# Weight-conversion steps held near TensorE's count, a logarithm moved behind a relu, and a last output tile in two halves

## The chip, the cores and the metric

The kernel runs on one core of one Trainium2 chip. The metric is the time of one execution on the device, in microseconds (us), as the median over runs. Each engine of the core (TensorE, written PE; VectorE, DVE; ScalarE, ACT; GpSimd, POOL; SyncE, SP) takes its instructions strictly in the order in which the program holds them, and waits at the front of that order until the semaphores that an instruction needs have come.

## The reference

Attention with a threshold, two Fourier transforms, a two-layer MLP and a gated output, for 4 batches of 576 tokens and 512 features:

```python
attn = softmax over the scores >= max - tau          # 8 heads of 64
x = (attn @ v), heads side by side                   # [4, 576, 512]
u = x + real(fft(fft(x, axis=1), axis=2))
un = (u - mean(u)) / sqrt(var(u) + 1e-6)
y = u + maximum(un @ w_ch1, 0) @ w_ch2               # 512 -> 2048 -> 512
gate = sigmoid(causal convolution of y, 5 taps)
out = (gate * (y @ w_val)) @ w_out
```

## The kernel before

All matrix products of the MLP and of the output are done three times over in a 12-bit-mantissa format (high part times high part, high times low, low times high), so each operand stands as a pair `h`, `l`. The two parts come from ScalarE (the high part: a copy or a relu) and VectorE (the low part: the value less the high part).

The MLP runs over tokens in five chunks (512, 384, 512, 512, 384 columns). Chunks 2 and 3 (`FAST`) take the first layer by a seven-product scheme for 2x2 blocks: `g_fast` (L1252) makes eight passes `p`, and a pass has seven products of six matmuls of 256 columns each, into PSUM tiles `x`, `y` and `zz`. The products are tied to each other by small ScalarE and VectorE instructions: `copied` (L1312, ScalarE) takes a partial sum out of PSUM into a scratch half `tmp` before the next product adds to it, `added` (L1316, VectorE) adds a second partial sum, and `relu` (L1323 on ScalarE for `hh`, L1324 on VectorE for `hl`) makes the hidden activations of one half. In the traces `tmp[0]` and `tmp[1]` are both called `cx`, `tmp[2]` is `ct`; some of the `hh`/`hl` pairs lie in tiles called `cx`/`ct` too. Between the products stand the matmuls of the second layer (L1279, three of 512 columns into `c`), taken from a queue by `fill(k)`: eight such groups a pass, four for each hidden block. So a pass has 7 products and 8 groups, 15 steps of 1536 columns each.

`y` and `zz` lie in a pool of two PSUM banks (`ps_f`), and so does `mean`, the column sums for the layer norm (L1037). The norm of the chunk runs beside the passes: squares (L1081), sums on GpSimd (L1086, L1088), `mean`, then Ln and Exp on ScalarE (L1097 and L1098, each behind a table load), then L1100 to L1104 on VectorE, of which L1101 reads `mean`. `advance_norm` takes one step of it where `g_fast` yields, and the Ln only where it yields "long".

`moe2_w_val` and `moe2_w_out` arrive as 64-bit floats and are turned into pairs on the way, beside the passes: each of the pieces that fall into chunks 2 and 3 is loaded by GpSimd's queue into `raw` (L966), converted by L281, L282 (VectorE), L283, L284 (ScalarE), L285, L286, L287 (VectorE) and L291 (GpSimd), and written back to memory from GpSimd's queue (L992). These are the conversion steps.

Where they stand among the instructions of the passes is decided while the program is built: a planner (`Loom`) holds a clock `loom.now[e]` for each engine, every matmul of a pass moves PE's clock on, and at a yield of `g_fast` the main loop lets the planner place all conversion steps whose start is not beyond PE's clock:

```python
                    loom.run(until=loom.now["PE"])
```

The results of a chunk are finished by `g_finish` (L1159: L1164 on VectorE reads `c`, L1165 on GpSimd adds to `res`, L1167 writes to `y_d`); for a chunk ahead of a fast one its four parts are taken one by one at yields of the next chunk's `g_fast`. At the end `emit_out` (L1819) makes 18 output tiles of 128 tokens: twelve matmuls of 512 columns, one ScalarE copy, one write on SP's queue.

Of the kernel before, what the change touches and what calls it, by code (L numbers as in the profile page):

```python
# [12 lines left out]
F32 = mybir.dt.float32  # L13
# [3 lines left out]
AF = mybir.ActivationFunctionType  # L17
# [5 lines left out]
B, H, S, D = 4, 8, 576, 64  # L23
DM = H * D
# [17 lines left out]
FAST = (2, 3)  # L42
# [832 lines left out]
def mlp(tc, right, ps_f, attention, loom, a, u_d, y_d, dram, wide, cw, out):  # L875
    nc = tc.nc
    PE, DVE, ACT, POOL, SP = nc.tensor, nc.vector, nc.scalar, nc.gpsimd, nc.sync
    KB, FB = DM // 128, DFF // 128
# [5 lines left out]
    with ExitStack() as ctx, ExitStack() as top, ExitStack() as top2:  # L884
# [3 lines left out]
        w, got = {}, {}  # L888
# [363 lines left out]
        def g_fast(c):  # L1252

            n = CHUNKS[c]
            m = n // 2
            T = {k: [t.rearrange("p (a b) -> p a b", a=2)[:, :, 0:m] for t in v] for k, v in t_units().items()}
            if c == FAST[0]:
                hb[:] = [[got["h"].tile([128, NM], F32R, tag=f"h{x}", name=f"h{x}") for x in "hl"] for _ in range(2)] + [[units["third"].tile([128, NM], I32, tag=t, name=t).bitcast(F32R) for t in ("cx", "ct")]]
            tmp = [f32(t)[:, i * 256:i * 256 + m] for t in units["cv"][2:] for i in range(2)]
            over, end = [], False  # L1260
            x0 = FAST.index(c) * FB

            def fill(k):
                for _ in range(k):
                    if q:
                        q.popleft()()
                        loom.now["PE"] += 3 * (n / 2.4 + 13.5)

            def group(p, jx, x, o):
                hh, hl = hb[(x0 + x) % 3]  # L1270
                w2h, w2l = w[jx][1]
                first, last = x == 0, x == FB - 1

                def go():
                    if first and o == 0:
                        finish_rest(left[0])
                        ch[c] = [got["ps_c"].tile([128, 512], F32, tag=f"c{o}", name=f"c{o}") for o in range(KB)]
                    for i, (ww, y) in enumerate(((w2h, hh), (w2l, hh), (w2h, hl))):
                        PE.matmul(out=ch[c][o][:, 0:n], lhsT=ww[:, o * 128:(o + 1) * 128], rhs=y[:, 0:n],  # L1279
                                  start=(first and i == 0), stop=(last and i == 2))  # L1280
                    if last:
                        whole.append(o)
                return go

            def product(f, wt, name, first):
                wh, wl = wt
                i = 0
                th, tl = T[name]
                for ww, x in ((wh, th), (wl, th), (wh, tl)):
                    for k in range(2):  # L1290
                        PE.matmul(out=f[:, 0:m], lhsT=ww[:, k * 128:(k + 1) * 128], rhs=x[:, k], start=(first and i == 0),  # L1291
                                  stop=(i == 5), skip_group_check=not first)
                        i += 1
                loom.now["PE"] += 6 * (m / 2.4 + 11.5)
                over.append(name)

            later = []

            def settle():
                while later:  # L1300
                    relu(*later.pop(0))
                while over:
                    name = over.pop(0)
                    if end and c + 1 in FAST:
                        split_block(c + 1, name)

            def taken(ns, e):
                loom.now[e] = max(loom.now[e], loom.now["PE"] - 2000.0) + ns

            def copied(f, t):  # L1310
                taken(act(m), "ACT")
                ACT.activation(t, f[:, 0:m], AF.Copy)  # L1312

            def added(f, t):
                taken(dve(m), "DVE")
                DVE.tensor_tensor(out=t, in0=f[:, 0:m], in1=t, op=ALU.add)  # L1316
                return t

            def relu(src, x, half):
                hh, hl = (t[:, half * m:half * m + m] for t in hb[(x0 + x) % 3])  # L1320
                taken(act(m), "ACT")
                taken(dve(m), "DVE")
                ACT.activation(hh, src, AF.Relu)  # L1323
                DVE.scalar_tensor_tensor(out=hl, in0=src, scalar=0.0, in1=f32(hh), op0=ALU.max, op1=ALU.subtract)  # L1324

            base = (FAST.index(c)) * FB * 2
            for p in range(FB // 2):
                lo, up = w[p][0], w[p + FB // 2][0]
                a11, a12, a22 = ([t[:, i:i + 256] for t in tt] for tt, i in ((lo, 0), (lo, 256), (up, 256)))
                k0 = base + 4 * p  # L1330
                for i in (p, min(p + 2, FB // 2 - 1)):
                    loom.run(lambda: ("combined", i) in loom.done)
                fetch(k0 + 5)
                s2, s1, s3, s4 = ([units["x"][:, (k0 + i) % 5, x:x + 256] for x in (0, 256)] for i in range(4))
                end = p == FB // 2 - 1
                if end and c + 1 in FAST:
                    yield "blocks"
                x = got["ps_h"].tile([128, 512], F32, tag="h", name="x")
                product(x, a11, "b11", True)
                copied(x, tmp[0])  # L1340
                settle()
                yield
                y = ps_f.tile([128, 512], F32, tag="f", name="y")
                product(y, a12, "b21", True)
                added(y, tmp[0])
                later.append((tmp[0], 2 * p, 0))
                yield
                fill(1)
                yield
                product(x, s2, "t2", False)  # L1350
                copied(x, tmp[1])
                settle()
                fetch(k0 + 6)
                yield
                z = ps_f.tile([128, 512], F32, tag="f", name="zz")
                product(z, s1, "t1", True)
                copied(z, tmp[2])
                settle()
                fetch(k0 + 7)
                yield  # L1360
                fill(1)
                yield
                product(x, s3, "t3", False)
                added(x, tmp[2])
                settle()
                fetch(k0 + 8)
                yield "long"
                fill(2)
                relu(tmp[2], 2 * p + 1, 1)
                yield  # L1370
                product(z, s4, "b22", False)
                added(z, tmp[1])
                later.append((tmp[1], 2 * p, 1))
                fetch(k0 + 9)
                yield
                fill(1)
                yield
                product(x, a22, "t4", False)
                settle()
                later.append((x[:, 0:m], 2 * p + 1, 0))  # L1380
                yield
                fill(3)
                yield
                for i, jx in enumerate((p, p + FB // 2)):
                    q.extend(group(p, jx, 2 * p + i, o) for o in range(KB))
            settle()
            rest[:] = [lambda: fill(2 * KB)]

        rest = []
        q, hb, whole, left = deque(), [], [], [iter(())]  # L1390
# [257 lines left out]
        for c in range(1, NCH):  # L1648
            last = c == NCH - 1
            if c in FAST:  # L1650
                norm = g_var(c, POOL)
                for n, m in enumerate(g_fast(c)):
                    if whole and (n % 2 or c > FAST[0]):
                        whole.pop(0)
                        next(left[0], None)
                        continue
                    if n < 12:
                        continue
                    loom.run(until=loom.now["PE"])
                    if m == "blocks":  # L1660
                        while not centred:
                            advance_norm(c, True)
                    advance_norm(c, table=m == "long")
# [66 lines left out]
def gate_out(tc, y_d, w_d, cw, out, ps_f, ypad0, gate0):  # L1730
# [4 lines left out]
    KB = DM // 128  # L1735
    PAD = NK - 1
    with ExitStack() as ctx:
# [79 lines left out]
        flat = out.rearrange("b s f -> (b s) f")  # L1817

        def emit_out(t):  # L1819
            f = ps_o.tile([128, DM], F32, tag="o", name="o")  # L1820
            gh, gl = gv[t * 128 // (2 * S)]
            d = slice(t * 128 % (2 * S), t * 128 % (2 * S) + 128)
            i = 0
            for x, w in ((gh, wo[0]), (gh, wo[1]), (gl, wo[0])):
                for k in range(KB):
                    PE.matmul(out=f, lhsT=x[:, k, d], rhs=w[:, k], start=(i == 0), stop=(i == 3 * KB - 1))  # L1826
                    i += 1
            s = o_p.tile([128, DM], F32, tag="os", name="os")
            ACT.activation(s, f, AF.Copy)
            SP.dma_start(out=flat[t * 128:t * 128 + 128], in_=s)  # L1830

        ps_v = ps_f
        load_y(0)
# [165 lines left out]
```

## Time and profile before

| | |
|---|---|
| median of 3 runs | 847.61 us (847.33 to 848.21) |
| the profiled execution, its own time | 846.86 us |
| its span, first to last instruction | 845.1 us |
| mean granted TensorE clock | 0.998 of full speed |

Busy shares of the span, from the page of the profile: PE 96%, DVE 75%, ACT 53%, POOL 47%. A busy time is what an engine spent inside instructions; where one engine is busy for nearly the whole span, what counts is its idle stretches and what ended each of them, and the stage in which they lie. The stages by time: attention and Fourier transforms to about 400 us, the MLP's chunks to about 740 us (chunk 2 from 492.6, chunk 3 from about 578, chunk 4 from about 673), the gated output to the end.

### The profile page before, as it was taken

Reading aid. Unit: us, or ns where it says so; the run is one execution under the profiler, and the core shown is the slowest. Engines: PE = TensorE matmul, PEld = TensorE weight load, DVE = VectorE, ACT = ScalarE, POOL = GpSimd, SP = SyncE. Lnnn points to the kernel's source line nnn. Section 1 sums busy time; section 2 is a strip of 40 time slices with the busy share of each in tenths; the row PEclk is TensorE's granted clock in tenths of the full one; section 3 lists DMA queues with packets and bytes.
Section 4 is the critical chain, followed back from the end, with each engine's and each line's share of the span. In section 5 each row is a group of like instructions: output and inputs, shape, how many; then the busy total and the mean of one; then the engine's idle time right before and its main releaser. Section 6 shows DMA issues by size and latency. Waiting matters only on the chain.

```text
span 845.1 us, 14968 instructions
## 1 busy us (share of the span) xinstructions
PE 812.5 (96%) x5164; PEld 657.7 (78%) x5164; DVE 633.1 (75%) x1378; ACT 450.5 (53%) x947; POOL 393.1 (47%) x464
## 2 busy tenths in 40 slices
PE   8989999999999999999999999899899999999998
PEld 6555556566665667878899988798799899999986
DVE  7999899898989998798789775756543475829730
ACT  5787787786778866544534254434443223243432
POOL 4557864796788567664242032412421101075421
PEclk9999999999999999999999999999999999999999
DMA  6367365355753459958645557366643141442111
GB/s 217 99 224 236 105 173 185 140 180 174 245 173 140 159 180 377 357 146 325 240 155 219 191 170 253 122 199 225 210 123 109 57 140 38 152 166 82 63 50 62
DMA packets 75435, 145.00 MB, mean 172 GB/s; under 512 B 14296, under 2 KB 24536, under 8 KB 75360
## 3 DMA queue, kind: packets, MB, share of 16 engines
q1 hardware_dynamic: 66736, 116.00, 40.4%
q0 software_dynamic: 8480, 28.05, 10.6%
q8 instruction: 41, 0.67, 0.3%
q14 instruction: 34, 0.28, 0.1%
q10 hardware_dynamic: 144, 0.00, 0.0%
HBM read 104.17 MB, written 39.86 MB: 170 GB/s over the span
## 4 chain that ended last, share of the span: by engine, by line
PE 69%; DVE 19%; ACT 5%; POOL 4%; issue 3%; DVEq 0%; POOLq 0%; ACTq 0%
PE c L1279 10%; PE h L1135 8%; PE c L1152 8%; DVE neg L766 6%; DVE p L783 6%; PE o L1826 5%; PE c L1553 5%; PE h L1517 5%; PE v L1808 5%; PE x L1291 5%; PE s L701 4%; PE f L458 4%; PE zz L1291 2%; PE t L803 2%; ACT e L772 2%
## 5 line engine op out<-in xcount | busy, mean ns | idle before, releaser
L791 POOL TENSOR_SCALAR p<-p,su 128x576 f32<-128x576 f32 x144 | 110.2, 775 | 83.9 <-DVE su L718 74.6
L772 ACT ACTIVATE e<-s,neg 128x576 f32<-128x576 f32 x144 | 102.1, 742 | 50.6 <-DVE neg L766 43.9
L783 DVE SCALAR_TENSOR_TENSOR p<-s,thr,e 128x576 f32<-128x576 f32 x144 | 112.4, 814 | 8.7 <-DVE thr L711 0.5
L766 DVE TENSOR_REDUCE neg<-s 128x1 f32<-128x576 f32 x144 | 102.4, 746 | 5.6 <-PE s L701 5.0
L701 PE MATMUL s<-kt,qt 64*128 64x288 f32 (+1 forms) x640 | 98.3, 438 | 6.9 <-DVE p L783 5.6
L701 PEld LDWEIGHTS s<-kt,qt 64*128 64x128 f32 (+1 forms) x640 | 45.7, 175 | 46.2 <-issue 15.6
L803 PE MATMUL t<-ident,p 128*128 128x128 f32 x464 | 68.9, 280 | 8.9 <-ACT m L820 6.6
L803 PEld LDWEIGHTS t<-ident,p 128*128 128x128 f32 x464 | 50.6, 140 | 30.1 <-issue 13.7
L458 PE MATMUL f<-m,v 128*64 128x320 f32 (+1 forms) x512 | 69.5, 411 | 0.0
L820 ACT ACTIVATE m<-t 128x512 f32<-128x512 f32 x116 | 65.6, 599 | 1.6 <-PE t L803 0.7
L1138 ACT ACTIVATE hh<-h 128x384 fp32r<-128x384 f32 x32 | 15.7, 491 | 81.4 <-PE h L1135 81.3
L291 POOL TENSOR_TENSOR ct<-raw 128x512 fp32r<-128x512 f32 x24 | 26.0, 1083 | 69.6 <-DVE raw L287 40.0
L1165 POOL TENSOR_TENSOR res<-cs,res 128x512 f32<-128x512 f32 (+1 forms) x16 | 19.5, 1243 | 77.9 <-DVE cs L1164 77.9
L458 PEld LDWEIGHTS f<-m,v 128*64 128x64 f32 x512 | 33.8, 137 | 27.3 <-ACT m L820 3.5
L1782 DVE SCALAR_TENSOR_TENSOR acc<-ypad,cw,acc 128x288 f32<-128x288 f32 x96 | 42.9, 513 | 0.0
L1152 PE MATMUL c<-hl,w1h 128*128 128x384 f32 x128 | 42.8, 334 | 0.0
L1152 PE MATMUL c<-hh,w1l 128*128 128x384 f32 x128 | 42.8, 334 | 0.0
L1152 PE MATMUL c<-hh,w1h 128*128 128x384 f32 x128 | 42.8, 334 | 0.0
L1811 DVE TENSOR_TENSOR gvf<-v,gate 128x288 f32<-128x288 f32 x30 | 13.6, 454 | 36.7 <-PE v L1808 35.5
L1312 ACT ACTIVATE cx<-x 128x256 f32<-128x256 f32 x32 | 12.2, 382 | 49.7 <-PE x L1291 49.7
L1139 DVE SCALAR_TENSOR_TENSOR hl<-h,hh 128x384 fp32r<-128x384 f32 x32 | 17.8, 555 | 27.6 <-ACT hh L1138 27.6
L283 ACT ACTIVATE cx<-cx,wide_bias 128x512 int32<-128x512 int32 x40 | 28.9, 722 | 14.3 <-DVE cx L281 14.2
(349 smaller groups left out, 2240.9 us busy)
## 6 DMA issues: line engine op xcount, KB each, us to landing
raw<-in_moe_w_ch POOLq DMA_DIRECT2D x32, 512.0 KB, 5.9
mlp_xu<-s SPq DMA_DIRECT2D x64, 256.0 KB, 3.7
qt<-in_q SPq DMA_DIRECT2D x15, 576.0 KB, 5.2
kt<-in_k SPq DMA_DIRECT2D x15, 432.0 KB, 3.7
s<-raw SPq DMA_DIRECT2D x12, 512.0 KB, 2.6
ypad<-y_d SPq DMA_DIRECT2D x16, 288.0 KB, 3.1
out<-os SPq DMA_DIRECT2D x18, 256.0 KB, 2.0
v<-in_v SPq DMA_DIRECT2D x16, 256.0 KB, 2.6
```

The source lines that it names most:

```text
L458: PE.matmul(out=f[h * 64:h * 64 + 64, 0:n], lhsT=w, rhs=r, start=(t == 0), stop=(t == 4))
L701: PE.matmul(out=s[o, c, 0:HALF], lhsT=qt[w, hh, q], rhs=kt[w, 2 if h == 2 and hh else hh], start=True, stop=True)
L766: DVE.tensor_reduce(out=neg[u][:, j, 0:1], in_=sc[g][:, :, 0:HALF], axis=AX.XY, op=ALU.max, negate=True)
L772: ACT.activation(e, sc[g][:, :, 0:HALF], AF.Exp, bias=neg[u][:, j, 0:1], scale=1.0)
L783: DVE.scalar_tensor_tensor(out=p_view(g).rearrange("p (a b) -> p a b", a=2), in0=sc.pop(g)[:, :, 0:HALF], scalar=thr[u][:, j:j + 1], in1=e ...
L791: POOL.tensor_scalar(out=v, in0=v, scalar1=ssum[u][:, j:j + 1], scalar2=1.0, op0=ALU.mult, op1=ALU.mult)
L803: PE.matmul(out=f[:, t, :], lhsT=pv[:, t * 128:(t + 1) * 128], rhs=ident, is_transpose=True, start=(t == 0), stop=(t == 3))
L820: ACT.activation(o, fv, AF.Copy)
L1135: PE.matmul(out=f[:, 0:n], lhsT=ww[:, k * 128:(k + 1) * 128], rhs=x[:, k, 0:n], start=(i == 0), stop=(i == 3 * KB - 1))
L1152: PE.matmul(out=ch[c][o][:, 0:n], lhsT=ww[:, o * 128:(o + 1) * 128], rhs=x, start=(at_ == 0 and i == 0), stop=(at_ == FB - 1 and i == 2))
L1279: PE.matmul(out=ch[c][o][:, 0:n], lhsT=ww[:, o * 128:(o + 1) * 128], rhs=y[:, 0:n], start=(first and i == 0), stop=(last and i == 2))
L1291: PE.matmul(out=f[:, 0:m], lhsT=ww[:, k * 128:(k + 1) * 128], rhs=x[:, k], start=(first and i == 0), stop=(i == 5), skip_group_check=not f ...
```

## The change

Three edits. First, at each yield of `g_fast` that takes a step of the norm or lets the planner run, the planner's clocks of DVE, ACT and POOL are moved up to no earlier than PE's clock less 700 ns, so that conversion steps are not placed as if those engines had been free long before; and the four parts of the chunk-1 finish are taken at the yields numbered 5, 6, 7, 8 of the first fast chunk, where they were taken at 1, 3, 5, 7. Second, the yield called "long", at which the Ln may be placed, moves behind the relu of `tmp[2]`. Third, the last output tile is made in two halves of 256 columns, each with its own copy and write.

```diff
                 added(x, tmp[2])
                 settle()
                 fetch(k0 + 8)
-                yield "long"
+                yield
                 fill(2)
                 relu(tmp[2], 2 * p + 1, 1)
-                yield
+                yield "long"
                 product(z, s4, "b22", False)
...
                 for n, m in enumerate(g_fast(c)):
-                    if whole and (n % 2 or c > FAST[0]):
+                    if whole and (n > 4 or c > FAST[0]):
                         whole.pop(0)
                         next(left[0], None)
                         continue
+                    for e in ("DVE", "ACT", "POOL"):
+                        loom.now[e] = max(loom.now[e], loom.now["PE"] - 700.0)
                     if n < 12:
                         continue
                     loom.run(until=loom.now["PE"])
...
         def emit_out(t):
-            f = ps_o.tile([128, DM], F32, tag="o", name="o")
             gh, gl = gv[t * 128 // (2 * S)]
             d = slice(t * 128 % (2 * S), t * 128 % (2 * S) + 128)
-            i = 0
-            for x, w in ((gh, wo[0]), (gh, wo[1]), (gl, wo[0])):
-                for k in range(KB):
-                    PE.matmul(out=f, lhsT=x[:, k, d], rhs=w[:, k], start=(i == 0), stop=(i == 3 * KB - 1))
-                    i += 1
             s = o_p.tile([128, DM], F32, tag="os", name="os")
-            ACT.activation(s, f, AF.Copy)
-            SP.dma_start(out=flat[t * 128:t * 128 + 128], in_=s)
+            n = DM // 2 if t == B * S // 128 - 1 else DM
+            for r in (slice(r, r + n) for r in range(0, DM, n)):
+                f = ps_o.tile([128, DM], F32, tag="o", name="o")[:, 0:n]
+                i = 0
+                for x, w in ((gh, wo[0]), (gh, wo[1]), (gl, wo[0])):
+                    for k in range(KB):
+                        PE.matmul(out=f, lhsT=x[:, k, d], rhs=w[:, k, r], start=(i == 0), stop=(i == 3 * KB - 1))
+                        i += 1
+                ACT.activation(s[:, r], f, AF.Copy)
+                SP.dma_start(out=flat[t * 128:t * 128 + 128, r], in_=s[:, r])
```

The order of the built programs shows what this moves. The first place (place A) is VectorE at the start of chunk 2, pass 0, where the four L1164 finish chunk 1:

```order
 L1316 TENSOR_TENSOR cx<-y,cx 128x256
+L1324 SCALAR_TENSOR_TENSOR hl<-cx,hh 128x256
 L1164 TENSOR_TENSOR cs<-c_5568,nr 128x384
-L1324 SCALAR_TENSOR_TENSOR hl<-cx,hh 128x256
+L1316 TENSOR_TENSOR ct<-x,ct 128x256
 L1164 TENSOR_TENSOR cs<-c_5569,nr 128x384
+L1324 SCALAR_TENSOR_TENSOR hl<-ct,hh 128x256
 L1164 TENSOR_TENSOR cs<-c_5570,nr 128x384
-L1316 TENSOR_TENSOR ct<-x,ct 128x256
-L1324 SCALAR_TENSOR_TENSOR hl<-ct,hh 128x256
+L1316 TENSOR_TENSOR cx<-zz,cx 128x256
 L1164 TENSOR_TENSOR cs<-c_5571,nr 128x384
```

Before, three L1164 stood ahead of the first `ct<-x`; now one does, and each instruction of the pass stands between two L1164.

The second place (place B) is ScalarE and VectorE in the pass of chunk 2 that holds the Ln. ScalarE before:

```order
L1312 ACTIVATE ct<-zz 128x256
L283 ACTIVATE cx<-cx,wide_bias 128x512
L284 ACTIVATE ct<-ct 128x512
L1097 ACT_TABLE_LOAD
L1097 ACTIVATE nr<-mean,eps 128x512
L1098 ACT_TABLE_LOAD
L1098 ACTIVATE nr<-nr 128x512
L1323 ACTIVATE hh<-ct 128x256
L1323 ACTIVATE hh<-cx 128x256
L1312 ACTIVATE cx<-x 128x256
```

ScalarE now:

```order
L1312 ACTIVATE ct<-zz 128x256
L1323 ACTIVATE hh<-ct 128x256
L1097 ACT_TABLE_LOAD
L1097 ACTIVATE nr<-mean,eps 128x512
L1098 ACT_TABLE_LOAD
L1098 ACTIVATE nr<-nr 128x512
L283 ACTIVATE cx<-cx,wide_bias 128x512
L1323 ACTIVATE hh<-cx 128x256
L284 ACTIVATE ct<-ct 128x512
L1312 ACTIVATE cx<-x 128x256
```

`hh<-ct` has passed the Ln block, and the two conversion steps have gone from in front of the block to behind it. VectorE in the same pass, before:

```order
L1316 TENSOR_TENSOR ct<-x,ct 128x256
L1324 SCALAR_TENSOR_TENSOR hl<-ct,hh 128x256
L285 SCALAR_TENSOR_TENSOR cx<-raw,cx 128x512
L286 SCALAR_TENSOR_TENSOR raw<-raw,ct 128x512
L287 TENSOR_SCALAR raw<-cx 128x512
L1316 TENSOR_TENSOR cx<-zz,cx 128x256
L1100 TENSOR_TENSOR cs<-nr 128x512
L1101 SCALAR_TENSOR_TENSOR cs<-mean,eps,cs 128x512
L1324 SCALAR_TENSOR_TENSOR hl<-cx,hh 128x256
```

VectorE now:

```order
L1316 TENSOR_TENSOR ct<-x,ct 128x256
L1324 SCALAR_TENSOR_TENSOR hl<-ct,hh 128x256
L281 TENSOR_SCALAR cx<-raw 128x512
L1316 TENSOR_TENSOR cx<-zz,cx 128x256
L282 TENSOR_SCALAR ct<-raw 128x512
L1324 SCALAR_TENSOR_TENSOR hl<-cx,hh 128x256
L285 SCALAR_TENSOR_TENSOR cx<-raw,cx 128x512
L286 SCALAR_TENSOR_TENSOR raw<-raw,ct 128x512
L1100 TENSOR_TENSOR cs<-nr 128x512
L1101 SCALAR_TENSOR_TENSOR cs<-mean,eps,cs 128x512
```

`cx<-zz` has now one conversion step in front of it in place of three, and L1100 and L1101 stand behind the relu `hl<-cx` and two conversion steps.

The third place (place C) is ScalarE in pass 1 of chunk 3, where L1081 takes the chunk's squares:

```order
 L1323 ACTIVATE cx<-x 128x256
-L283 ACTIVATE cx<-cx,wide_bias 128x512
-L284 ACTIVATE ct<-ct 128x512
 L1081 ACTIVATE cs<-z 128x512
 L1312 ACTIVATE cx<-x 128x256
 L1323 ACTIVATE hh<-cx 128x256
+L283 ACTIVATE cx<-cx,wide_bias 128x512
+L284 ACTIVATE ct<-ct 128x512
 L1312 ACTIVATE ct<-zz 128x256
```

The two conversion steps have moved from in front of the copy `cx<-x` to in front of the copy `ct<-zz`.

## Rows read from the trace of the kernel before

**Rows 1.** The page: each engine's busy time, share of the span, instructions.
```profile
PE 812.5 (96%) x5164; PEld 657.7 (78%) x5164; DVE 633.1 (75%) x1378; ACT 450.5 (53%) x947; POOL 393.1 (47%) x464
```

**Rows 2.** TensorE's waits, 430 to 680 us: total, times, longest (us).
```profile
PE x L1291 <- ACT cx L1312: 2.9, 1, 2.9
PE c L1279 <- DVE hl L1324: 1.1, 1, 1.1
PE y L1291 <- DVE cx L1316: 1.0, 1, 1.0
PE x L1291 <- DVE ct L1316: 0.9, 1, 0.9
PE c L1279 <- ACT hh L1323: 0.4, 1, 0.4
PE zz L1291 <- ACT ct L1312: 0.3, 1, 0.3
```

**Rows 3.** Busy time by stretch: PE, PEld, DVE, ACT, POOL (instructions), PEclk, DMA, GB/s.
```profile
530.00:550.00 20.00, 17.64 (x107) 15.04 (x106) 15.48 (x28) 7.49 (x19) 9.57 (x11) 1.00 0.40 120
590.00:610.00 20.00, 17.14 (x99) 15.04 (x98) 10.09 (x20) 8.54 (x20) 9.46 (x9) 0.91 0.65 211
610.00:630.00 20.00, 20.00 (x128) 18.06 (x128) 10.68 (x22) 9.00 (x18) 5.10 (x6) 1.00 0.38 112
```

**Rows 4.** Timeline, VectorE at place A: start, length, line, tiles, [idle before].
```profile
495.63 0.95 DVE L1324 SCALAR_TENSOR_TENSOR hl<-cx,hh 128x256 fp32r<-128x256 f32 x1 [0.43 <-ACT hh L1323]
496.50 1.01 DVE L1164 TENSOR_TENSOR cs<-c,nr 128x384 f32<-128x384 f32 x2
497.43 0.41 DVE L1316 TENSOR_TENSOR ct<-x,ct 128x256 f32<-128x256 f32 x1
```

**Rows 5.** Timeline at place B: ScalarE, VectorE, and TensorE's `y`.
```profile
527.00 1.28 ACT L1097 ACT_TABLE_LOAD   x1
...
530.29 0.63 ACT L1098 ACTIVATE nr<-nr 128x512 f32<-128x512 f32 x1
530.83 0.40 ACT L1323 ACTIVATE hh<-ct 128x256 fp32r<-128x256 f32 x1
...
531.27 0.43 DVE L1324 SCALAR_TENSOR_TENSOR hl<-ct,hh 128x256 fp32r<-128x256 f32 x1 [4.45 <-ACT hh L1323]
531.61 0.69 DVE L285 SCALAR_TENSOR_TENSOR cx<-raw,cx 128x512 int32<-128x512 int32 x1
...
533.15 0.42 DVE L1316 TENSOR_TENSOR cx<-zz,cx 128x256 f32<-128x256 f32 x1
...
535.00 0.75 DVE L1101 SCALAR_TENSOR_TENSOR cs<-mean,eps,cs 128x512 f32<-128x512 f32 x1
...
533.62 0.51 PE L1291 MATMUL y<-raw,w0h 128*128 128x256 f32 x2 [1.03 <-DVE cx L1316]
```

**Rows 6.** Timeline at place C: VectorE, ScalarE, and TensorE's `x`.
```profile
592.30 1.49 DVE L282 TENSOR_SCALAR ct<-raw 128x512 int32<-128x512 int32 x1
...
592.41 0.72 ACT L283 ACTIVATE cx<-cx,wide_bias 128x512 int32<-128x512 int32 x1 [2.75 <-DVE cx L281]
593.82 0.63 ACT L284 ACTIVATE ct<-ct 128x512 f32<-128x512 int32 x1 [0.69 <-DVE ct L282]
...
594.88 0.36 ACT L1312 ACTIVATE cx<-x 128x256 f32<-128x256 f32 x1
...
595.29 0.75 PE L1291 MATMUL x<-unh,mlp_xu 128*128 128x256 f32 x4 [2.86 <-ACT cx L1312]
```

**Rows 7.** The last output tile: its copy in the timeline, and the writes' landing.
```profile
841.48 0.60 ACT L1829 ACTIVATE os<-o 128x512 f32<-128x512 f32 x1 [2.19 <-PE o L1826]
...
DMA to landing us min/median/max: 2.0/2.0/2.2
```

**Rows 8.** Line L281, 490 to 675 us: duration ns min/median/max, and idle before it.
```profile
L281 DVE TENSOR_SCALAR cx<-raw x8: 417/422/812, 489.6 to 607.3; 128x512 int32<-128x512 int32 x8
...
  DMA moe_w_val_h<-cx: 2.0, 1
```

## The prediction

> **What bounds the kernel now.** I read the busy shares first: TensorE is busy 96% of the span [rows 1], so only what makes it wait, or run at a lower clock, can move the time. Next its waits in the two fast chunks [rows 2]: six, of 2.9, 1.1, 1.0, 0.9, 0.4 and 0.3 us, together 6.6. The table by stretch puts a price on them [rows 3]. A regular stretch of 20 us holds 128 matmuls, so one is worth 0.156 us. A pass has 66 of them (7 products of 6, 8 groups of 3), so it takes 10.3 us, and one of its 15 steps 0.70. The stretch 530 to 550 holds 107, which is 21 x 0.156 = 3.3 us lost, where the waits show 1.0 + 1.1 + 0.3 = 2.4: a stall costs some 0.3 us beyond what is shown. The stretch 590 to 610 holds 99, which is 4.5 us lost for one wait of 2.9; there the granted clock reads 0.91 where the others read 1.00, so about 18% of it ran at the lower level (1.2 of 2.4 GHz), worth 9% of 20 us = 1.8. At place A the waits of 0.9 and 0.4, with 0.3 each, make 1.9 us. The three places lose 9.7 us in all. The rest of the change stands where TensorE does not wait, apart from the end.
>
> **Place A, start of chunk 2.** TensorE's `x` waited 0.9 [rows 2] for `ct<-x`, which ran from 497.43 to 497.84 [rows 4]; so it was due at about 497.0. Ahead of it VectorE held `hl<-cx`, 0.95, with GpSimd's L1165 at work beside it (the same form takes 0.43 [rows 5]), and three L1164, two of them 1.01 together [rows 4]. Now `hl<-cx` comes first, at 495.63 and without L1165 beside it, as no L1164 has yet fed GpSimd: it ends at 496.06, one L1164 (0.5) at 496.6, `ct<-x` (0.41) at 497.0. The 0.9 goes. The second wait has two L1164 and a contended `hl<-ct` behind `ct<-x` still ahead of `cx<-zz`, and so of `hh<-cx`. It was 0.4; I take 0.65, as an L1164 of 0.5 has come between, less half of it in slack. Left: 0.65 + 0.3 = 0.95, gain 0.9. Bounds: from nothing (the two L1164 at 0.95 each, as contended as the relu) to all 1.9.
>
> **Place B, the Ln in chunk 2.** ScalarE's Ln block runs from 527.00, and `hh<-ct` behind it begins at 530.83: 3.83 us [rows 5]. VectorE idles 4.45 us for it, does the conversion steps L285 to L287 from 531.61, and only then `cx<-zz` at 533.15, for which `y` waits 1.03 until 533.62 [rows 5]; so `y` was due at 532.6. Now `hh<-ct` and `cx<-zz` need nothing of the block. `hh<-ct` goes when TensorE has left the buffer that it writes: that is where the product `zz` begins, seven steps ahead of `y`, 532.6 - 7 x 0.70 = 527.7. Behind its 0.40 the block begins at 527.9 (neighbours overlap by 0.1 to 0.2) and lets the next instruction go at 531.7. `cx<-zz` runs near 529, so the 1.03 goes. L283 (0.72 [rows 6]) and `hh<-cx` (0.40) end at 532.8, `hl<-cx` (0.43) at 533.2. TensorE wants `hh` one step behind `y`, at 533.3, and `hl` at 533.8: no wait, with 0.5 of slack.
>
> What is late next is L1101, since `mean` keeps one of the two banks of `ps_f` until it has been read, and the next `zz` needs that bank. TensorE wants it three steps behind `y`, at 534.7. Behind `hl<-cx` stand L285 and L286 (0.69 for the first [rows 5]; 1.2 for both, as they overlap a little: the three before took 533.15 - 531.61 = 1.54, the last a short one), then L1100, at 0.7 like L285, then L1101, 0.75 [rows 5]: 533.2 + 1.2 + 0.65 + 0.75 = 535.8. A new wait of 1.1 therefore, with the 0.3 a loss of 1.4 in place of 3.3: gain 1.9. L1100 takes two inputs from memory, and such an operation has been seen to double beside GpSimd (0.43 to 0.95, [rows 4, 5]); then L1101 comes 0.8 later. Bounds: nothing (the wait grows to the old loss) to 2.9 (GpSimd idle, small overlaps).
>
> The block's length decides here. The two loads and two activations fit into the 3.83 us, since from the first load (1.28) to the second activation (530.29) only 3.29 pass [rows 5]. The Trainium skill (ScalarE: Activation LUTs, "What ACT_TABLE_LOAD costs") gives each switch of tables a load of about 1283 ns and then a drain of about 1380. The load agrees with the row. Two drains would not fit between those two starts, so the trace speaks against them, and I use the row; by the Trainium skill the block would end 2.76 later, and both Ln would lose about that much.
>
> **The Ln of chunk 3.** It made no wait before. The same shift applies, with no conversion steps left in front of L1100. Against place B the chain is shorter by L283, L285 and L286, about 1.2 at VectorE, which is the wait of place B: the loss is 0.1, between 0 and 0.8.
>
> **Place C, chunk 3.** The copy `cx<-x` began at 594.88, and `x` waited 2.86 until 595.29 [rows 6]: due at 592.43. Ahead of it stood L283, for which ScalarE had idled 2.75 from 589.66, L284, held by L282 (1.49), and L1081. Without the first two ScalarE is free early: L1081 and the copy (0.36) end near 591.5, before 592.43. The wait of 2.86 goes, and I take the clock's fall to go with it: the stretch 530 to 550 had a stall of 1.06 and read 1.00 [rows 2, 3], this one had 2.86 and read 0.91. Now L284 stands ahead of `ct<-zz`. It ended at 594.45, the copy behind it ends at 594.8, and the product that needs it is due three steps behind 592.43, at 594.5: a wait of 0.3, of which I count 0.4. Gain 4.5 - 0.4 = 4.1. Bounds: 2.3 (that wait at 2, with no fall of the clock) to 4.5.
>
> **The last tile.** Before: twelve matmuls of 512, a copy of 0.60, a write that lands in 2.0 to 2.2 [rows 7]. Now the last copy has 256 columns, 0.36 like the copy in rows 6, and the first half's copy and write run beside TensorE's second half. The second write goes through the same queue behind the first; its landing I leave as it is. Gain 0.2, between 0 (a landing that grows by as much) and 0.5 (the lesser write is quicker).
>
> **The order's other moves.** Clamping the clocks lets conversion steps go later, not more often. GpSimd's loads (L966) and writes (L992) and its step L291 go with them; SP's queue holds no conversion work. I cost them at nothing: the cover is the slack of the pieces, whose loads wait in `raw`. The one place where it was thin is the rival that ends slower.
>
> **Sum.** 0.9 + 1.9 - 0.1 + 4.1 + 0.2 = 7.0 us. The profiled execution took 846.86, which gives 839.9; it lies 0.75 below the median of 847.61, from which the same gain gives **840.6 us**.
>
> **The rivals.** About 0.2%, or 1.7 us, is what a measurement of this kernel can tell from no change.
>
> 1. At place C the wait only moves: L282, 1.49 because GpSimd works beside it, holds L284 later by as much, and the wait at `zz` is 1.8 with the clock's fall again: 1.8 + 0.3 + 1.8 = 3.9 in place of 0.4. Gain 3.5, **844.1**. For it: L282 now runs later among other steps. Against: the wait would begin from a point where TensorE has not idled yet, and be shorter than 2.86.
>
> 2. At place B L1100 and the steps ahead of it double beside GpSimd, and `zz` waits 3.0, as much as was lost before: gain 5.1, **842.5**. For it: GpSimd is busy 9.57 of 20 us in this stretch [rows 3]. Against: none of VectorE's steps in rows 5 was doubled.
>
> 3. No change: the block is longer in its new place. If each load took its 1.28 twice, `hl<-cx` would come 2.6 later at both Ln, less the slack of 0.5 in the first, a loss of 2.1 + 2.6 and some stalls: gain about 1.7, **845.9**. Against: the length in rows 5 was taken with the same neighbours. The drain that the Trainium skill names, above, would end at about the same time.
>
> 4. The gain is given back: something behind chunk 3 ends at a fixed time, a transfer or a chain of VectorE's, and TensorE waits there for what it won. About **847**. Against: TensorE is the bound to the end, and no wait in rows 2 is on a transfer.
>
> 5. Slower: the conversion steps wait on transfers. L281 once idled 2.0 us for the write of the piece before [rows 8], harmlessly, since VectorE had time. Now L281 is placed late and stands just ahead of `added` steps such as `cx<-zz`; a write that has not landed would hold the whole pass. Eight conversions fall into the two chunks [rows 8]. To be slower by 1.7 us it must eat the 7.0 as well, 8.7 in all: from 1.1 us of held TensorE per conversion on. At 1.5 each the loss is 12, **852.6**. For it: the 2.0 is seen. Against: once in eight, and a later L281 leaves the write more time.
>
> **How the numbers follow.** Chances: my forecast 0.63, with its own range 838.5 to 842 (from the bounds at A and B); rival 1 0.12; rival 2 0.11; rival 3 0.03; rival 4 0.05; rival 5 0.06. The range goes down to 837.8 (B at 2.9, A and C whole, a tail of 0.5: 9.8 gained) and up to 844.2, which takes in rivals 1 and 2 and leaves out 3 to 5, 0.14, and the outer ends of the bounds. Faster by over 0.2%: the forecast and rivals 1 and 2, 0.86; within 0.2%: rivals 3 and 4, 0.08; slower: rival 5, 0.06.
>
> **What would show it.** Right: among TensorE's waits the 2.9 on the copy `cx`, the 1.0 on `cx<-zz` and the 0.9 on `ct<-x` are gone; a new one of about 1.1 at `zz` for L1101, one near 0.65 at place A, one near 0.3 for `ct<-zz` at place C; the stretches at places B and C hold about 119 and 125 matmuls, with a granted clock of 1.00 in the second; the last copy takes 0.36. Wrong: TensorE's waits name `hl` or `hh` behind the Ln block (rival 3), L281 idles for transfers ahead of an `added` (rival 5), the clock falls again at place C (rival 1), or the waits go and the span keeps its length through new ones behind 680 us (rival 4).

## The result and the profile after

The changed kernel takes 840.02 us (median of 5 runs, 839.31 to 842.30) where the kernel before takes 847.61: the ratio is 0.9913, 95% interval 0.9899 to 0.9928. The forecast was 840.6, in a range of 837.8 to 844.2. The profiled execution is the slowest of the five, 842.30, with a span of 840.5 us: it lost 2.3 us near 220 us, in the attention stage, where its granted clock read 0.50 from 220 to 222 us and 0.68 to 224; that stage's order of work is the same in both kernels. So I don't compare spans, but the moments at which TensorE begins the same matmul in the two traces:

| TensorE's matmul | before, us | after, us | after less before |
|---|---|---|---|
| `y`, last pair, first pass of chunk 2 | 493.73 | 496.87 | +3.14 |
| `zz`, behind place A | 505.80 | 507.78 | +1.98 |
| `c<-cx`, ahead of place B | 530.33 | 532.11 | +1.78 |
| `zz`, behind place B | 548.71 | 548.74 | +0.03 |
| `y`, ahead of place C | 589.22 | 589.20 | -0.02 |
| `c<-cx`, behind place C | 599.99 | 595.85 | -4.14 |
| first `h` of chunk 4 | 673.06 | 669.08 | -3.98 |
| `o` of an output tile | 832.86 | 828.87 | -3.99 |
| end of the span | 845.1 | 840.5 | -4.6 |

From 3.14 behind to 4.6 ahead are 7.7 us: 1.16 at place A and 0.2 more by 515 us, 1.75 at B, 4.1 at C, 0.6 at the end, less 0.16 in the pass of chunk 3's Ln; nothing between 673 and 832 us.

Of TensorE's waits from 430 to 680 us two are left [rows 2]:

```profile
PE zz L1291 <- DVE cs L1101: 1.2, 1, 1.2
PE zz L1291 <- ACT ct L1312: 0.3, 1, 0.3
```

The stretches of places B and C (columns as in [rows 3]) hold 118 and 123 matmuls, 11 and 24 more, and the second has its clock back:

```profile
530.00:550.00 20.00, 18.84 (x118) 16.76 (x117) 14.02 (x25) 10.31 (x22) 6.67 (x7) 1.00 0.44 133
...
590.00:610.00 20.00, 19.72 (x123) 17.37 (x122) 14.02 (x27) 9.23 (x21) 9.28 (x9) 1.00 0.71 233
```

Place A in the timeline of VectorE [rows 4]: the relu takes 0.43, `ct<-x` stands behind one L1164, and the relu `hl<-ct` takes 0.56. The relu `hl<-cx` behind them takes 0.85, and TensorE's `c<-hl` starts 0.54 behind the matmul ahead of it, where 0.24 is usual: a stall of 0.3, too short for the list above (VectorE, then TensorE):

```profile
498.77 0.43 DVE L1324 SCALAR_TENSOR_TENSOR hl<-cx,hh 128x256 fp32r<-128x256 f32 x1 [0.90 <-ACT hh L1323]
499.11 0.55 DVE L1164 TENSOR_TENSOR cs<-c,nr 128x384 f32<-128x384 f32 x1
499.58 0.42 DVE L1316 TENSOR_TENSOR ct<-x,ct 128x256 f32<-128x256 f32 x1
...
500.48 0.56 DVE L1324 SCALAR_TENSOR_TENSOR hl<-ct,hh 128x256 fp32r<-128x256 f32 x1
...
502.33 0.85 DVE L1324 SCALAR_TENSOR_TENSOR hl<-cx,hh 128x256 fp32r<-128x256 f32 x1
...
502.69 0.40 PE L1279 MATMUL c<-hh,w1l 128*128 128x512 f32 x1
503.23 0.50 PE L1279 MATMUL c<-hl,w1h 128*128 128x512 f32 x1
```

Place B [rows 5], ScalarE, VectorE and TensorE: the block gives way to L283 at 533.53, `hl<-cx` runs at 534.58, L1101 ends at 537.60, and `zz` begins behind it:

```profile
533.53 0.71 ACT L283 ACTIVATE cx<-cx,wide_bias 128x512 int32<-128x512 int32 x1
534.14 0.40 ACT L1323 ACTIVATE hh<-cx 128x256 fp32r<-128x256 f32 x1
...
534.58 0.43 DVE L1324 SCALAR_TENSOR_TENSOR hl<-cx,hh 128x256 fp32r<-128x256 f32 x1 [3.43 <-ACT hh L1323]
...
536.85 0.75 DVE L1101 SCALAR_TENSOR_TENSOR cs<-mean,eps,cs 128x512 f32<-128x512 f32 x1
...
537.65 0.74 PE L1291 MATMUL zz<-unh,mlp_xu 128*128 128x256 f32 x4 [1.16 <-DVE cs L1101]
```

The prediction gave L1100 0.7 us. In the kernel before it had taken 1.48, beside L291 on GpSimd, in lines that [rows 5] leaves out:

```profile
533.48 1.48 DVE L1100 TENSOR_TENSOR cs<-nr 128x512 f32<-128x512 f32 x1
...
533.38 1.04 POOL L291 TENSOR_TENSOR ct<-raw 128x512 fp32r<-128x512 f32 x1 [14.28 <-DVE raw L287]
```

In the changed kernel it takes 0.69, and L291 comes 2 us behind it:

```profile
536.12 0.69 DVE L1100 TENSOR_TENSOR cs<-nr 128x512 f32<-128x512 f32 x1
...
538.74 1.09 POOL L291 TENSOR_TENSOR ct<-raw 128x512 fp32r<-128x512 f32 x1 [15.19 <-ACT cx L1323]
```

Place C [rows 6]: L284 still waits for L282, but now only `ct<-zz` stands behind it:

```profile
593.83 0.63 ACT L284 ACTIVATE ct<-ct 128x512 f32<-128x512 int32 x1 [0.71 <-DVE ct L282]
594.37 0.36 ACT L1312 ACTIVATE ct<-zz 128x256 f32<-128x256 f32 x1
...
594.79 0.75 PE L1291 MATMUL zz<-unh,mlp_xu 128*128 128x256 f32 x4 [0.28 <-ACT ct L1312]
```

The last copy [rows 7] begins 3.0 us before the span's end, where the one before began 3.6 before it:

```profile
837.51 0.38 ACT L1833 ACTIVATE os<-o 128x256 f32<-128x256 f32 x1 [0.99 <-PE o L1831]
```

### The profile page after: what moved, and what is told of

Same layout as the page of the kernel before. It is cut to its first block, busy times and chain, and to the rows that moved or that the text cites. A ratio compares the mean times of both kernels' runs of the same rounds, so it can differ in the third digit from the quotient of the medians.

```text
span 840.5 us, 14996 instructions
## 1 busy us (share of the span) xinstructions
PE 812.9 (97%) x5176; PEld 659.3 (78%) x5176; DVE 634.9 (76%) x1378; ACT 451.1 (54%) x948; POOL 394.3 (47%) x464
## 4 chain that ended last, share of the span: by engine, by line
PE 70%; DVE 17%; ACT 5%; POOL 3%; issue 3%; DMA 1%; SPq 0%; DVEq 0%; ACTq 0%; POOLq 0%
PE c L1279 10%; PE h L1135 8%; PE c L1152 8%; DVE neg L766 6%; DVE p L783 6%; PE o L1831 5%; PE h L1517 5%; PE c L1553 5%; PE v L1810 5%; PE x L1291 5%; PE s L701 4%; PE f L458 4%; ACT e L772 3%; PE zz L1291 2%; PE t L803 2%
## 5 line engine op out<-in xcount | busy, mean ns | idle before, releaser
L291 POOL TENSOR_TENSOR ct<-raw 128x512 fp32r<-128x512 f32 x24 | 25.7, 1073 | 71.9 <-DVE raw L287 49.8
L283 ACT ACTIVATE cx<-cx,wide_bias 128x512 int32<-128x512 int32 x40 | 28.9, 722 | 11.7 <-DVE cx L281 11.7
L1279 PE MATMUL c<-hh,w1h 128*128 128x512 f32 x88 | 34.8, 395 | 0.0
```

## The experiments

My theory at the start: each place is paid by one edit, A by the yields 5 to 8, C by the clamp, the end by the halves; and at B either the clamp or the Ln's move would have been enough, and the two together get in each other's way. The rival: the Ln's move is what pays at B, and the wait for L1101 is its price. The kernel before ran again beside the experiments, with medians of 848.11 us (e_n4 to e_noln), 847.72 (b_late to t_onewrite) and 847.24 (the last three); the ratios are to these, while the expected times start from 847.6.

**e_n4: only the finish's yields**, on the kernel before.

```diff
-                    if whole and (n % 2 or c > FAST[0]):
+                    if whole and (n > 4 or c > FAST[0]):
```

> Only the four L1164 of chunk 1 go to the later yields. Theory: place A is theirs alone, so this kernel gains what the changed kernel gained there, 1.4 us (846.2), with both waits of place A gone and those of places B and C as before (1.03, 1.06, 2.86). Rival: place A was also helped by the clamped clocks, and the second wait, 0.4, stays: gain 0.7, 846.9.

Measured: 846.95 us (ratio 0.9990, interval 0.998 to 1.000); in the trace 1.16 us are gained at place A, as in the changed kernel, but 0.5 given back 13 us later. L281 idles 2.0 for its transfer as in [rows 8], L282 0.6 more, and ScalarE's L284 holds the copy `cx<-x`, which TensorE now wants earlier:

```profile
511.22 0.43 DVE L281 TENSOR_SCALAR cx<-raw 128x512 int32<-128x512 int32 x1 [1.98 <-DMA moe_w_val_h<-cx]
512.25 0.43 DVE L282 TENSOR_SCALAR ct<-raw 128x512 int32<-128x512 int32 x1 [0.60 <-DMA moe_w_val_l<-ct]
...
512.71 0.63 ACT L284 ACTIVATE ct<-ct 128x512 f32<-128x512 int32 x1 [0.30 <-DVE ct L282]
513.25 0.36 ACT L1312 ACTIVATE cx<-x 128x256 f32<-128x256 f32 x1
...
513.66 0.74 PE L1291 MATMUL x<-unh,mlp_xu 128*128 128x256 f32 x4 [0.44 <-ACT cx L1312]
```

So the rival's size was right (0.65 net in the trace) and its reason wrong: place A needs no clamp, but the clamp keeps what A has won. This is my rival 5 in small, 0.4 us of held TensorE at one conversion.

**e_clamp: only the clamp**, on the kernel before.

```diff
+                    for e in ("DVE", "ACT", "POOL"):
+                        loom.now[e] = max(loom.now[e], loom.now["PE"] - 700.0)
```

> Only the clocks are clamped. Theory: place C is the clamp's alone (gain 4.0), and at place B it is the conversion steps that did the harm, not the place of the Ln: with L283 and L284 no longer in front, the block begins 1.3 us earlier, hh<-ct follows it at 529.6, cx<-zz comes by 531.2 and L1101 ends by 533.2, all before TensorE asks, so all 3.3 us of place B are gained as well: 7.3 in all, 840.3, with no wait at y, c or zz there. Rival: the block in front of hh<-ct still makes y or c wait, some 1.5 us of it: 841.8 or more, with such a wait among TensorE's.

Measured: 840.70 us (0.9913, 0.9899 to 0.9927). Place B gained 3.2 of 3.3, with no wait at `y`, `c` or `zz`: VectorE has `cx<-zz` at 531.83 and L1101 at 533.22, in a trace that runs 1.6 us behind that of before at this point.

```profile
530.72 0.40 ACT L1323 ACTIVATE hh<-ct 128x256 fp32r<-128x256 f32 x1
...
531.83 0.42 DVE L1316 TENSOR_TENSOR cx<-zz,cx 128x256 f32<-128x256 f32 x1
...
533.22 0.75 DVE L1101 SCALAR_TENSOR_TENSOR cs<-mean,eps,cs 128x512 f32<-128x512 f32 x1
```

Place C gained its 4.1. But 0.95 went between the two, in waits that I had not expected, told under e_noln. By its ratio the clamp alone is as good as the whole change, 0.9913 each; by the traces it gains 6.6 us from chunk 2 to the end, where the whole change gains 7.7.

**e_ln: only the Ln's move**, on the kernel before.

```diff
-                yield "long"
+                yield
                 fill(2)
                 relu(tmp[2], 2 * p + 1, 1)
-                yield
+                yield "long"
```

> Only the Ln moves behind the relu. Theory: L283 and L284 stay in front of the block and so out of the way of hh<-cx behind it; hl<-cx ends at 532.6 and L1101 at 533.95, before zz asks at 534.7: place B is gained whole, 3.3 us, 844.3, with place A and C as before. Rival (the wait for the bank of mean comes of the Ln's new place as such): zz waits 1.2 for L1101 as in the changed kernel, gain 1.75, 845.9.

Measured: 843.44 us (0.9947, 0.9935 to 0.9960); place B gained 3.2 and its waits are gone, and places A and C are as before. TensorE's waits from 430 to 690 us:

```profile
PE x L1291 <- ACT cx L1312: 2.9, 1, 2.9
PE x L1291 <- DVE ct L1316: 0.9, 1, 0.9
PE c L1279 <- ACT hh L1323: 0.4, 1, 0.4
```

The rival falls: with the Ln behind the relu, L1101 started at 533.17 here and nothing waited for it. The wait of 1.16 in the changed kernel comes of both edits: the clamp puts L283 behind the block and L285, L286 behind `hl<-cx`, where the moved Ln has no slack left for them.

**e_noln: the changed kernel without the Ln's move.**

```diff
-                yield
+                yield "long"
                 fill(2)
                 relu(tmp[2], 2 * p + 1, 1)
-                yield "long"
+                yield
```

> The changed kernel without the move of the Ln. Theory: the move costs 1.5 us beside the clamp (two good edits that get in each other's way): place B has no wait left, and the time is 1.5 to 1.8 under the changed kernel's 840.0, 838.4; ratio to before 0.989. Rival: without the move y, c or zz wait 1 us or more at place B, and the time is 840.0 or above.

Measured: 839.71 us (0.9901, 0.9889 to 0.9914). Place B is gained whole, 3.15 in place of 1.75, but one pass later 0.95 is lost: the next chunk's `mean` stands where it stood before, four steps ahead of its place in the changed kernel, and TensorE, now earlier, meets it while L1026 and L1027 still make its two parts.

```profile
542.36 0.50 PE L1037 MATMUL mean<-cs,ones 128*128 128x512 f32 x1 [0.21 <-ACT cs L1026]
...
543.08 0.50 PE L1037 MATMUL mean<-cs,ones 128*128 128x512 f32 x1 [0.22 <-DVE cs L1027]
```

Two waits shown with 0.2 each cost 0.95 by the matmuls' start times. So the Ln's move had an effect that I had not seen in the order: as every later step of the norm goes with it, it also gave `mean` its distance.

**b_late: e_noln with a later `mean`.**

```diff
-            yield 2500.0 if c > FAST[0] else 4500.0
+            yield 4500.0
             mu = col_mean(parts)
```

> The changed kernel without the move of the Ln, and the step from the sums to mean made 4500 ns long in the fast chunks (was 2500). Theory: of the 1.55 us that the version without the move gained at place B, 0.95 was given back one pass later, where mean now stood right behind the sums' two parts and TensorE waited for L1026 and L1027; three steps later it finds them done: 0.95 under that version, 838.7, and none of the two waits at mean. Rival: a later mean holds its bank longer and another product waits for it, so that the time stays at 839.7.

Measured: 838.94 us (0.9891, 0.9878 to 0.9904). The waits at `mean` are gone, and from chunk 2 to the end this trace gains 9.0 us on that of before, where the changed kernel gains 7.7 and e_noln 8.4. By the traces it beats these two; by the medians it is 1.1 us under the changed kernel, with intervals that overlap.

**x_bank: the changed kernel, with `mean` copied out of PSUM ahead of the Ln.**

```diff
             yield "table"
+            if c in FAST:
+                v = scratch(n)
+                DVE.tensor_copy(v, var)
             ACT.activation(r, var, AF.Ln, bias=eps[:, 0:1])
+            if c in FAST:
+                var = v
```

> The changed kernel, in which VectorE copies mean out of PSUM just ahead of the Ln, and L1101 reads the copy. Theory: what is left at place B is the bank of ps_f that mean holds until L1101; with the copy ended by 531.5 the zz product, due at 536.5, gets its bank early, the wait of 1.16 for L1101 goes, and the time is 1.3 to 1.5 under the changed kernel's: 838.6, with no wait in its place. Rival: the late Ln block makes something else late as well (hl<-x or cx<-y behind L1100 and L1101 on VectorE), another wait of about 1 comes up in that pass, and the time stays at 839.5 to 840.

Measured: 839.51 us (0.9902, 0.9888 to 0.9917). The wait for L1101 is gone, and TensorE comes out of place B 1.35 us earlier than in the changed kernel; so it was the bank. Then 0.95 is lost again by 546 us, so that the rival's time held, by another instruction than it named: VectorE's relu `hl<-ct`, 0.43 in the kernel before, takes 3.24 with GpSimd's sums beside it, and `cx<-zz` and all behind it come late (VectorE, GpSimd and the weight load that waits at the end of the chain):

```profile
539.23 3.24 DVE L1329 SCALAR_TENSOR_TENSOR hl<-ct,hh 128x256 fp32r<-128x256 f32 x1 [0.55 <-ACT hh L1328]
542.40 0.41 DVE L1321 TENSOR_TENSOR cx<-zz,cx 128x256 f32<-128x256 f32 x1
...
539.62 2.56 POOL L1046 TENSOR_TENSOR cs<-z 128x512 f32<-128x512 f32 x2
...
543.32 0.19 PEld L1284 LDWEIGHTS c<-cx,w1h 128*128 128x128 f32 x1 [0.32 <-ACT cx L1328]
```

The relu ends at 542.47, just behind the two sums (542.18). The Trainium skill (SBUF — State Buffer, "SBUF: two separate sides") says that a VectorE instruction with two inputs from SBUF and a GpSimd one that reads SBUF don't share but exclude each other for a whole instruction, and that the one that starts first goes first. The end of the relu agrees; its start does not, since the record has it 0.39 ahead of the sums and it still waited for both. In the changed kernel the same relu took 3.15 and nobody waited, as I read it because TensorE was late from its wait for L1101: of the 1.35 that x_bank won there, 0.95 had been cover.

```profile
541.68 3.15 DVE L1324 SCALAR_TENSOR_TENSOR hl<-ct,hh 128x256 fp32r<-128x256 f32 x1 [0.64 <-ACT hh L1323]
```

That L1046 is the cause is read from the records, and they don't all agree. In e_ln the sums are done by 535.7, and this relu, at 538.91, takes 0.42. But in e_noln it takes 0.43 in the middle of the sums (GpSimd, then VectorE), so that standing beside them is not enough, and what decides stays open:

```profile
536.90 2.90 POOL L1046 TENSOR_TENSOR cs<-z 128x512 f32<-128x512 f32 x2
...
538.22 0.43 DVE L1324 SCALAR_TENSOR_TENSOR hl<-ct,hh 128x256 fp32r<-128x256 f32 x1 [0.68 <-ACT hh L1323]
```

**e_tail: only the halves**, on the kernel before (the third edit of the change, its line of sizes shown), and **t_onewrite**: the changed kernel, with one write behind both copies.

```diff
+            n = DM // 2 if t == B * S // 128 - 1 else DM
+            for r in (slice(r, r + n) for r in range(0, DM, n)):
```

```diff
                 ACT.activation(s[:, r], f, AF.Copy)
-                SP.dma_start(out=flat[t * 128:t * 128 + 128, r], in_=s[:, r])
+            SP.dma_start(out=flat[t * 128:t * 128 + 128], in_=s)
```

> Only the last tile in two halves. Theory: from the start of the last copy to the end of the span 2.99 us as in the changed kernel (3.62 before): 0.22 for the copy and 0.4 for the write of half the size; 847.0. Rival: the write of a half takes as long as that of a whole tile and the 0.4 was chance: 3.4 us, 847.4.

> The changed kernel with both halves' copies, but one write of the whole tile behind the second. Theory: the write's size is worth 0.4, so from the start of the last copy to the end of the span 3.4 us in place of 2.99; 840.4. Rival: only the copy counts, 3.0 us, and the time is the changed kernel's.

Measured: e_tail 847.21 us (0.9991, 0.9981 to 1.0002), t_onewrite 840.12 (0.9909, 0.9896 to 0.9922); the times can't tell this size, the traces can. The last copies are

```profile
841.93 0.38 ACT L1831 ACTIVATE os<-o 128x256 f32<-128x256 f32 x1 [0.99 <-PE o L1829]
```

in e_tail, whose span ends 3.0 behind, as in the changed kernel, and

```profile
834.98 0.38 ACT L1833 ACTIVATE os<-o 128x256 f32<-128x256 f32 x1 [0.99 <-PE o L1831]
```

in t_onewrite, whose span ends 3.4 behind. In the four kernels with the whole tile (before, e_n4, e_clamp, e_ln) it was 3.6. So 0.2 is the copy and 0.4 the write: here a write of 128 KB was done some 0.4 us before one of 256 KB.

**a_cl1500: the changed kernel with 1500 ns in the clamp.**

```diff
-                        loom.now[e] = max(loom.now[e], loom.now["PE"] - 700.0)
+                        loom.now[e] = max(loom.now[e], loom.now["PE"] - 1500.0)
```

> The changed kernel with the clocks moved up to TensorE's less 1500 ns in place of 700. In its order ScalarE has L283 and L284 back in front of L1081 and of the copy at place C, and in front of the Ln block at place B. Theory: place C waits 2.9 for that copy again and mostly loses the clock with it (4.0 lost), while place B is gained whole as in the kernel with the Ln's move alone: 847.6 - 1.4 - 3.2 - 0.6 = 842.4. Rival: place C's gain is not the order's there but comes of lighter traffic or of VectorE's later steps, and the wait stays away: 838.5.

Measured: 842.36 us (0.9948, 0.9933 to 0.9963). The 2.86 at place C is back, with L283 and L284 in front of the copy, and place B has no wait (the other 0.3 is at the start of chunk 3):

```profile
PE x L1291 <- ACT cx L1312: 3.2, 2, 2.9
```

The clock did not fall in this profile, though the wait is the same:

```profile
590.00:600.00 10.00, 7.34 (x44) 6.54 (x45) 4.79 (x9) 4.91 (x11) 5.51 (x7) 1.00 0.69 189
```

That puts a price on the clock alone: past place C this trace is 1.55 us better off than that of before. The same difference stands in e_n4 and e_tail, whose profiles had the wait and a clock of 1.00 there too. So the time agrees with the theory's 842.4 partly by luck: the trace kept the 1.55 that the theory gave up, and lost 0.6 at the start of chunk 3, of which it had nothing.

**b_cl300: b_late with 300 ns**, and **b_384**: b_late with the last tile cut into 384 and 128 columns.

```diff
-                        loom.now[e] = max(loom.now[e], loom.now["PE"] - 700.0)
+                        loom.now[e] = max(loom.now[e], loom.now["PE"] - 300.0)
```

```diff
-            n = DM // 2 if t == B * S // 128 - 1 else DM
-            for r in (slice(r, r + n) for r in range(0, DM, n)):
+            cuts = (0, 384, DM) if t == B * S // 128 - 1 else (0, DM)
+            for r in (slice(*x) for x in zip(cuts, cuts[1:])):
```

> The version with the late mean and the Ln where it was before, with 300 ns in place of 700. In its order L283 and L284 stand behind the copy ct<-zz at place C. Theory: the last wait of place C (0.28, some 0.6 with what follows) goes, and TensorE waits nowhere over 0.3 in the fast chunks: 0.3 to 0.8 under 838.9, 838.4. Rival: later conversion steps meet GpSimd's sums or the loads, and a wait of another kind takes its place: 838.9 or above.

> The version with the late mean and the Ln where it was before, the last tile cut into 384 and 128 columns in place of two halves. Theory: the copy of 128 columns takes 0.11 less than that of 256, the write of 64 KB some 0.2 less than that of 128 KB, so that from the start of the last copy to the end of the span 2.7 us pass where the halves take 2.99: 838.6. Rival: TensorE's twelve matmuls of 128 columns are held by their weight loads, 0.11 apart instead of 0.06, which costs 0.6 and eats it: 839.2.

Measured: b_cl300 838.54 us (0.9905, 0.9888 to 0.9921). Place C gains all of 4.7, and 1.2 is lost in the pass of chunk 3's Ln, in a wait that no other kernel has:

```profile
618.78 0.50 PE L1279 MATMUL c<-hl,w1h 128*128 128x512 f32 x1 [0.75 <-DVE hl L1324]
```

From chunk 2 to the end it gains 8.6, less than b_late's 9.0: the rival's mechanism held, though the time lies nearer to the theory's 838.4; the two times, 838.54 and 838.94, can't tell. b_384: 838.81 (0.9901, 0.9887 to 0.9915). Both guesses of what the pieces take held. The copy of 128 columns takes 0.28 and the span ends 2.7 behind its start; but four matmuls of 128 columns take 0.42 where four of 256 take 0.47, so that the twelve cost 0.55 more than half of what twelve of 256 take.

```profile
833.10 0.56 PE L1831 MATMUL o<-woh,gv1h 128*128 128x128 f32 x4
833.50 0.61 PE L1831 MATMUL o<-wol,gv1h 128*128 128x128 f32 x4
833.94 0.61 PE L1831 MATMUL o<-woh,gv1l 128*128 128x128 f32 x4
834.59 0.28 ACT L1833 ACTIVATE os<-o 128x128 f32<-128x128 f32 x1 [0.75 <-PE o L1831]
```

By these, the cut loses 0.3 against two halves.

## Why the prediction was right

The sum was 7.0 and the trace gives 7.7. The mechanism of each step held; two terms were mis-sized (the second wait of place A and the last write), and one was right for a reason that the prediction did not give (L1100 at place B).

- **Place A: 0.9 forecast, 1.16 measured.** `ct<-x` came when I had placed it. Of the second wait, for which I left 0.65 + 0.3, only short stalls remain, the longest the 0.3 at `c<-hl`: by the matmuls' starts 0.7 of the place's 1.9 is still lost, where I left 0.95. I took the relu `hl<-ct` as contended, as in the kernel before (1.05), and it took 0.56: the wait's term was mis-sized. The clamp holds what was won (e_n4). The 0.2 that follow by 515 us were not gained by t_onewrite, whose order is the same there, so I don't count them to this place.
- **Place B: 1.9 forecast, 1.75 measured.** The wait of 1.1 for L1101 came as 1.16. x_bank shows that it is the bank of `mean`. That L1100 took 0.69 was luck: I priced it like L285, while in the trace of before it took 1.48 beside L291, and my reason against rival 2, that no VectorE step there was doubled, held only for the lines that [rows 5] shows. It came out because L287 went later as well (538.17), and L291, which follows it, with it; with 1.48 the wait would have been some 0.8 longer (an estimate, 1.48 less 0.69). The block took 3.83 us from its first load (529.70) to L283, as before; the drain that the Trainium skill (ScalarE: Activation LUTs, "What ACT_TABLE_LOAD costs") puts behind a load shows in neither trace. What I did not see is that either edit alone takes the whole 3.2 (e_clamp, e_ln), though the order of each could have been read as that of both was: my steps took the change as one. In the whole change the Ln's move costs more than it brings: e_noln, without it, gains 8.4 in its trace where the changed kernel gains 7.7; the times can't tell these two apart.
- **The Ln of chunk 3:** 0.1 forecast, 0.16 measured, in a stall too short for the list.
- **Place C: 4.1 forecast, 4.1 measured,** the wait of 0.3 for `ct<-zz` included. The part that is the clock's is 1.55 rather than 1.8, and it hangs on more than the wait. Of the 43 runs of the kernel before that stand beside these experiments 40 read a mean clock of 0.998 or less (0.002 of the span is 1.7 us, about one such fall), as did 21 of 24 of e_n4 and e_tail, which keep the waits of places B and C; of e_ln and a_cl1500, which keep that of C and not those of B, 6 of 11 read 1.00. Of the changed kernel 4 of 5 do. A mean does not say where the clock fell: in the changed kernel's profiled run, which reads 0.998 too, it fell in the attention stage. What besides that wait brings the clock down stays open.
- **The end: 0.2 forecast, 0.6 measured.** I left the write's time as it was; the smaller write is quicker by 0.4 (t_onewrite): this term was mis-sized. It lay just beyond my bound of 0.5.
- **The rivals.** 1, 3 and 4 did not show. Of rival 2 a long relu beside GpSimd (3.15) was there, but one pass later, where nobody waited for it; of rival 5 a wait of 0.44 in e_n4, which the clamp removes.

## What to carry to other kernels

Where one engine is the bound and stalls for others at a few places, each place can be costed by when each instruction behind the move would end and when the bound engine asks for it; and after each gain ask what is late next, here the reader of a PSUM bank. Cost every edit alone as well as all together: two that each cure a place can spoil each other, and a wait can be the cover of the next one. Where a loss of less than a microsecond is in question, compare the start of the same matmul in two traces, since the times of whole runs scatter by more.

## What the runs showed that was not expected

A VectorE relu of 0.43 us took 3.24 (x_bank) and 3.15 (the changed kernel) while GpSimd added two tiles in 2.56 and 2.55; in e_noln, amid the same two sums, it took 0.43. Two waits of 0.2 us on a matmul of the column sums cost 0.95 together (e_noln). With the same stall of 2.86 us the clock fell in two profiles (before, e_ln) and not in three (a_cl1500, e_n4, e_tail); in the kernel before it fell behind the stall, which ended at 595.29: from 596 to 600 us it reads 0.57.
